# First-layer matmuls in alternation with the second layer of the preceding block, on a recurrence followed by a max-out MLP

## Chip, cores, metric

One Trainium2 chip, one core. The metric is the device time of one execution in microseconds (us), as a median of several runs. The kernel before took 483.24 us (482.63 to 483.64, 4 runs). All runs that are compared here were in the same, fast state with the matmul clock granted almost in full (a mean of 0.994 to 1.0 in every run), so nothing below depends on the clock.

## The reference

```python
# x, f_logit: [4, 6144, 256];  lower_bound: [256];  w1, w2: [256, 1024];  w_out: [1024, 256]
f = lower_bound + (1 - lower_bound) * sigmoid(f_logit)
h[t] = f[t] * h[t-1] + (1 - f[t]) * x[t]          # along the 6144 steps; y = all h
out = max(y @ w1, y @ w2) @ w_out                 # 24576 tokens
```

Both kernels use max(a, b) = a + relu(b - a): the output is relu(y @ (w2 - w1)) @ w_out + y @ (w1 @ w_out). The product w1 @ w_out ("w13", 256 x 256) is made once. I call y @ (w2 - w1) the **hidden** matmuls, y @ w13 the **base** matmuls, and the rest the **projection**.

## The kernel before

PE is the engine that does the matmuls, ACT the one for activations, DVE the vector engine. PSUM is the memory that matmuls write to; each kernel divides up eight banks of it. N is the number of columns that one matmul makes.

The kernel works on 48 blocks of 512 tokens. Per block PE does 16 transposes (x and f_logit come with tokens on the partitions, the recurrence needs them along the free dimension), 16 hidden matmuls (8 tiles dT of 128 x 512, two matmuls each), 8 base matmuls and 32 projection matmuls of N=256. ACT makes the sigmoid and, for each dT tile, the relu that frees the tile's PSUM buffer. DVE makes the gates, the scan and the copy of the output out of PSUM.

```python
    ps_t = ctx.enter_context(tc.tile_pool(name="ps_t", bufs=2, space=bass.MemoryType.PSUM))
    ps_d = ctx.enter_context(tc.tile_pool(name="ps_d", bufs=2, space=bass.MemoryType.PSUM))
    ps_o = ctx.enter_context(tc.tile_pool(name="ps_o", bufs=1, space=bass.MemoryType.PSUM))
    # ... (cut)
    def recurrence(j):
        # ... per half h of the 256 channels: 8 transposes into tT, then
            u = midpool.tile([P, TB], BF16, name="u")
            nc.scalar.activation(out=u[:], in_=fT, func=AF.Sigmoid, scale=-1.0)      # L174
            # ... ff = 1 + u * (lb - 1)                                              # L176
            nc.vector.scalar_tensor_tensor(out=v[:], in0=u[:], scalar=om[:, h : h + 1],
                in1=xT, op0=ALU.mult, op1=ALU.mult)                                  # L185
            # ... y = scan(ff, v)                                                    # L195

    def moe(j, w21, wob, w13b):
        # ...
        for fc in range(FC):                                       # 8 dT tiles
            dT = ps_d.tile([P, TB], FP32, name="dT")
            for kc in range(KC):
                nc.tensor.matmul(dT[:, :], lhsT=w21[:, kc, fc * P : (fc + 1) * P],
                    rhs=yk[kc][:, :], start=(kc == 0), stop=(kc == KC - 1))          # L213
            rt = rpool.tile([P, TB], BF16, name="rt")
            nc.scalar.activation(out=rt[:], in_=dT[:], func=AF.Relu)                 # L221
            rts.append(rt)
        psos = [ps_o.tile([P, D], FP32, name=f"psO{i}") for i in range(NSB)]   # 4 banks
        # ... base matmuls into psos                                                 # L226
        # ... projection: for fc, for i: psos[i] += rts[fc][:, i].T @ wob[fc]        # L235
        # ... one copy per psO, one store per pair                                   # L245

    for j in range(NBLK):
        if j + 2 < NBLK:
            load_nat(blocks[j + 2])
        if j + 1 < NBLK:
            recurrence(j + 1)
        moe(j, w21, wob, w13b)
```

PE's order inside this program is chosen by the scheduler; it puts the base matmuls between the hidden ones.

## Time and profile before

| what | value | view |
|---|---|---|
| time, span of the profiled run | 483.24 us, 481.1 us | runs, page |
| PE / DVE / ACT busy | 93% / 62% / 56% | page, part 1 |
| period of one block | 9.46 us (first osb copy 202.29, next block's 211.75) | timeline |
| PE work in a block, from starts of matmuls that wait for nothing | 16 x 0.2157 + 40 x 0.109 + 16 x 0.056 = 8.71 us | timeline |
| first hidden matmul, last matmul | 22.77 us, 476.28 us | timeline |

PE's 93% is no measure of how much is left. The Trainium skill, "Perfetto Trace Analysis", section "Identifying the Most-Contended Engine", says that matmul busy time is not a good measure of the distance to the limit, because pipelined instructions look smaller in a trace. The conclusion holds here, but in this trace they look longer: a matmul of N=512 is recorded as 0.38 us long, and the next one starts 0.215 us later. So count starts, not lengths.

The page of the kernel before: busy time, the chain that ended last, and groups (line, engine, operation, tiles | busy us, mean ns | idle before, releaser).

```profile
PE 448.3 (93%) x3440; PEld 309.0 (64%) x3488; DVE 296.2 (62%) x486; ACT 267.1 (56%) x500; POOL 71.9 (15%) x102
...
PE 65%; ACT 21%; issue 5%; DVE 5%; DMA 3%; SPq 0%; ACTq 0%; DVEq 0%
PE dT L213 27%; ACT rt L221 11%; ACT u L174 10%; DVE osb L245 4%; DMA won<-in_moe_w_out_dram 3%; PE dT L109 1%; PE psO_1331 L235 0%; PE psO_5231 L235 0%; PE psO_5101 L235 0%; PE psO_4971 L235 0%; PE psO_4451 L235 0%; PE psO_2631 L235 0%; PE
...
L221 ACT ACTIVATE rt<-dT 128x512 bf16<-128x512 f32 x384 | 214.2, 600 | 37.8 <-PE dT L213 36.9
...
L174 ACT ACTIVATE u<-tT 128x512 bf16<-128x512 bf16 x96 | 52.2, 595 | 153.9 <-DVE osb L245 150.0
...
L185 DVE SCALAR_TENSOR_TENSOR v<-u,om,tT 128x512 bf16<-128x512 bf16 x96 | 69.4, 723 | 0.0
```

The chain of work that ended last is 65% PE but 21% ACT: ACT is on the critical path although it is busy only 56% of the time.

The timeline of one hidden stage of the kernel before (start, duration, engine, line, instruction):

```profile
203.52 0.38 PE L213 MATMUL dT<-y_2586,w_144 128*128 128x512 bf16 x1
...
203.96 0.38 PE L213 MATMUL dT<-y_2586,w_144 128*128 128x512 bf16 x1
...
204.08 1.09 ACT L221 ACTIVATE rt<-dT 128x512 bf16<-128x512 f32 x2
204.17 0.27 PE L226 MATMUL psO_2758<-w13b,y_2569 128*128 128x256 bf16 x1
...
204.39 0.27 PE L226 MATMUL psO_2759<-w13b,y_2569 128*128 128x256 bf16 x1
...
204.74 0.38 PE L213 MATMUL dT<-y_2569,w_144 128*128 128x512 bf16 x1
```

PE starts hidden matmuls 0.215 us apart up to 203.96 (two of four are shown; the first has no record in the trace), then three base matmuls 0.11 us apart, the last at 204.39. That one is over at 204.50, but the next hidden matmul starts at 204.74: its dT tile is the third, and there are two buffers. The first relu (of the two in the 204.08 line) is what it waits for: it ends at 204.08 + 0.60 = 204.68. There are four such holes in this stage, of 0.24, 0.07, 0.19 and 0.26 us. They make up the 9.46 - 8.71 = 0.75 us per block. No bracket marks them behind PE, because a matmul is recorded longer than it holds up the next (a base matmul 0.27 us, a hidden one 0.38) and covers most of the hole after it. In the list of waits they stand with the weight loads, which waited for something that the profile does not name ("issue"):

```profile
engine line waited for: us in total, times, longest us
PEld L213 <- issue: 44.8, 192, 0.5
```

A table of one block (us of the stretch, then busy us and number of instructions of each engine, clock, DMA share, GB/s):

```profile
core 0: us, PE busy (x) PEld busy (x) DVE busy (x) ACT busy (x) POOL busy (x), PEclk, DMA share, GB/s
202.29:211.75 9.46, 9.20 (x73) 6.33 (x73) 6.08 (x11) 5.43 (x10) 1.48 (x2) 1.00 0.68 112
```

### The profile page before, as it was taken

The numbers are of one execution on the slowest core, as the hardware profiler recorded it, in microseconds if no ns is written. First come the engines' busy times: TensorE is split into PE (matmuls) and PEld (weight loads), VectorE is DVE, ScalarE is ACT, GpSimd is POOL, SyncE is SP. The second block draws the span as 40 slices with busy tenths as digits, with TensorE's granted clock in tenths as the row PEclk, the third lists the DMA queues.
The fourth block names the chain that finished last, engine by engine and source line by source line (L and its number), as shares of the span: only waits on it lengthen the run. The fifth ranks groups of instructions, "written<-read, shape, count | busy, mean of one in ns | idle before, by whom it ended". The sixth has DMA issues, their size and how long they took to land.

```text
span 481.1 us, 8867 instructions
## 1 busy us (share of the span) xinstructions
PE 448.3 (93%) x3440; PEld 309.0 (64%) x3488; DVE 296.2 (62%) x486; ACT 267.1 (56%) x500; POOL 71.9 (15%) x102
## 2 busy tenths in 40 slices
PE   0799999999999999999999999999999999999996
PEld 0566766676677667666766776676667666766663
DVE  2576577556756765676577567656765665577461
ACT  1666466546655664566466546655664565466553
POOL 4211121112111211211121112111111211120000
PEclk9999999999999999999999999999999999999999
DMA  9957567756765775677567757765785677465112
GB/s 246 191 99 121 90 119 120 113 87 131 118 104 89 136 119 96 102 138 111 90 124 115 114 89 133 118 102 99 130 122 90 120 116 116 89 115 106 46 45 87
DMA packets 78698, 54.06 MB, mean 112 GB/s; under 512 B 3392, under 2 KB 78144, under 8 KB 78656
## 3 DMA queue, kind: packets, MB, share of 16 engines
q0 software_dynamic: 50688, 25.17, 43.4%
q1 hardware_dynamic: 27968, 28.32, 19.6%
q8 instruction: 27, 0.44, 0.4%
q14 instruction: 15, 0.12, 0.1%
HBM read 53.48 MB, written 25.17 MB: 163 GB/s over the span
## 4 chain that ended last, share of the span: by engine, by line
PE 65%; ACT 21%; issue 5%; DVE 5%; DMA 3%; SPq 0%; ACTq 0%; DVEq 0%
PE dT L213 27%; ACT rt L221 11%; ACT u L174 10%; DVE osb L245 4%; DMA won<-in_moe_w_out_dram 3%; PE dT L109 1%; PE psO_1331 L235 0%; PE psO_5231 L235 0%; PE psO_5101 L235 0%; PE psO_4971 L235 0%; PE psO_4451 L235 0%; PE psO_2631 L235 0%; PE psO_1981 L235 0%; PE psO_4321 L235 0%; PE psO_2111 L235 0%
## 5 line engine op out<-in xcount | busy, mean ns | idle before, releaser
L221 ACT ACTIVATE rt<-dT 128x512 bf16<-128x512 f32 x384 | 214.2, 600 | 37.8 <-PE dT L213 36.9
L235 PEld LDWEIGHTS <-rt 128*128 128x128 bf16 x1536 | 150.0, 98 | 27.7
L174 ACT ACTIVATE u<-tT 128x512 bf16<-128x512 bf16 x96 | 52.2, 595 | 153.9 <-DVE osb L245 150.0
L213 PEld LDWEIGHTS <-w_144 128*128 128x128 bf16 x768 | 72.3, 97 | 81.8 <-issue 44.8
L140 POOL DMA_DIRECT2D xn<-in_x_dram x48 | 35.7, 744 | 356.3 <-PE tT L168 349.4
L185 DVE SCALAR_TENSOR_TENSOR v<-u,om,tT 128x512 bf16<-128x512 bf16 x96 | 69.4, 723 | 0.0
L162 PE MATMUL tT<-ident_b,xn 128*128 128x128 bf16 x384 | 37.5, 222 | 12.2 <-DMA xn<-in_x_dram 11.4
L176 DVE TENSOR_SCALAR ff<-u,lbm_94 128x512 bf16<-128x512 bf16 x96 | 46.3, 483 | 3.1 <-ACT u L174 1.6
L168 PE MATMUL tT<-ident_b,fn 128*128 128x128 bf16 x384 | 37.7, 221 | 1.2 <-DMA fn<-in_f_logit_dram 1.2
L162 PEld LDWEIGHTS <-xn 128*128 128x128 bf16 x384 | 27.9, 99 | 13.4 <-DMA xn<-in_x_dram 11.4
L144 POOL DMA_DIRECT2D fn<-in_f_logit_dram x48 | 35.9, 749 | 3.6 <-PE tT L168 2.3
L168 PEld LDWEIGHTS <-fn 128*128 128x128 bf16 x384 | 25.9, 99 | 1.5 <-DMA fn<-in_f_logit_dram 1.4
L101 ACT COPY w1T<-dT 128x128 bf16<-128x128 bf16 x16 | 3.0, 298 | 10.9 <-PE dT L94 10.9
L245 DVE COPY osb<-psO_6356 128x256 f32<-128x256 f32 x1 | 0.4, 425 | 7.2 <-PE psO_6356 L235 7.2
L79 DVE TENSOR_TENSOR w_144<-w2n,w1n 128x2048 bf16<-128x2048 f32 x1 | 2.3, 2293 | 2.7 <-DMA w2n<-in_moe_w_dram 2.7
L87 DVE CAST wob<-won 128x2048 bf16<-128x2048 f32 x1 | 1.2, 1228 | 3.8 <-DMA won<-in_moe_w_out_dram 3.8
L94 PE MATMUL dT<-ident_b,w1b 128*128 128x128 bf16 x16 | 2.2, 306 | 1.3 <-ACT w1T L101 1.2
L213 PE MATMUL dT<-y_121,w_144 128*128 128x512 bf16 x8 | 3.0, 377 | 0.3 <-ACT rt L221 0.2
L81 DVE CAST w1b<-w1n 128x2048 bf16<-128x2048 f32 x1 | 1.2, 1226 | 3.2 <-DMA w1n<-in_moe_w_dram 3.2
L213 PE MATMUL dT<-y_1269,w_144 128*128 128x512 bf16 x7 | 2.6, 377 | 0.5 <-ACT rt L221 0.4
L213 PE MATMUL dT<-y_5039,w_144 128*128 128x512 bf16 x7 | 2.6, 377 | 0.5 <-ACT rt L221 0.4
L213 PE MATMUL dT<-y_1286,w_144 128*128 128x512 bf16 x8 | 3.0, 378 | 0.1
(1066 smaller groups left out, 1034.3 us busy)
## 6 DMA issues: line engine op xcount, KB each, us to landing
out_dram<-osb SPq DMA_DIRECT2D x96, 256.0 KB, 2.4
xn<-in_x_dram POOLq DMA_DIRECT2D x48, 256.0 KB, 5.5
fn<-in_f_logit_dram POOLq DMA_DIRECT2D x48, 256.0 KB, 6.1
w1n<-in_moe_w_dram SPq DMA_DIRECT2D x1, 1024.0 KB, 5.2
w2n<-in_moe_w_dram SPq DMA_DIRECT2D x1, 1024.0 KB, 8.8
won<-in_moe_w_out_dram SPq DMA_DIRECT2D x1, 1024.0 KB, 14.4
lbc<-in_lower_bound_dram SPq DMA_DIRECT2D x1, 1.0 KB, 2.1
```

Source lines behind the costliest of these rows:

```text
L109: nc.tensor.matmul(psw[:, 0:D], lhsT=w1T[:, fc, kc * P : (kc + 1) * P], rhs=wob[:, fc, :], start=(fc == 0), stop=(fc == FC - 1),)
L140: nc.gpsimd.dma_start(out=xn[:], in_=x[blk.b, blk.t0 : blk.t0 + TB, :].rearrange("(i p) d -> p i d", p=P),)
L144: nc.gpsimd.dma_start(out=fn[:], in_=f_logit[blk.b, blk.t0 : blk.t0 + TB, :].rearrange("(i p) d -> p i d", p=P),)
L162: nc.tensor.transpose(tT[:, i * TSB : (i + 1) * TSB], blk.xn[:, i, h * P : (h + 1) * P], ident_b[:],)
L168: nc.tensor.transpose(tT[:, TB + i * TSB : TB + (i + 1) * TSB], blk.fn[:, i, h * P : (h + 1) * P], ident_b[:],)
L174: nc.scalar.activation(out=u[:], in_=fT, func=AF.Sigmoid, scale=-1.0)
L176: nc.vector.tensor_scalar(out=ff[:], in0=u[:], scalar1=lbm1[:, h : h + 1], scalar2=1.0, op0=ALU.mult, op1=ALU.add,)
L185: nc.vector.scalar_tensor_tensor(out=v[:], in0=u[:], scalar=om[:, h : h + 1], in1=xT, op0=ALU.mult, op1=ALU.mult,)
L213: nc.tensor.matmul(dT[:, :], lhsT=w21[:, kc, fc * P : (fc + 1) * P], rhs=yk[kc][:, :], start=(kc == 0), stop=(kc == KC - 1),)
L221: nc.scalar.activation(out=rt[:], in_=dT[:], func=AF.Relu)
L235: nc.tensor.matmul(psos[i][:, :], lhsT=rts[fc][:, i * TSB : (i + 1) * TSB], rhs=wob[:, fc, :], start=False, stop=(fc == FC - 1),)
L245: nc.vector.tensor_copy(out=osb[:, r, :], in_=psos[2 * g + r][:, :])
```

## The change

The intent: PE never runs one stage at a time. In each of eight slots it does one dT tile of block j, five matmuls (base or projection) of block j-1 and two transposes of block j+2, so that ACT has the whole slot for a relu. The PE order is fixed by the program. The gate scale (1 - lower_bound) moves out of v into the weights, so v becomes a plain product over both halves; sigmoid and output copy are merged too. Output pairs share a PSUM bank: banks go from 2 + 2 + 4 to 2 + 3 + 3 for transposes, dT and output. Inputs are loaded two blocks at a time, w_out is cast by its load, and weights come in halves from another queue.

The diff, cut to its core:

```diff
-    ps_t = ... bufs=2   ps_d = ... bufs=2   ps_o = ... bufs=1 (four names)
+    ps_t = ... bufs=1 (two names: fT, xT)   ps_d = ... bufs=3   ps_o = ... bufs=3 (one name)
 # recurrence: one instruction over both halves
-            nc.scalar.activation(out=u[:], in_=fT, func=AF.Sigmoid, scale=-1.0)      # 128x512, twice
-            nc.vector.scalar_tensor_tensor(out=v[:], in0=u[:], scalar=om[:, h : h + 1], in1=xT, ...)
+        nc.scalar.activation(out=u[:], in_=fT[:], func=AF.Sigmoid, scale=-1.0)       # 128x1024  L113
+        nc.vector.tensor_tensor(out=v[:], in0=u[:], in1=xT[:], op=ALU.mult)          # 128x1024  L115
 # weights
-        nc.vector.tensor_tensor(out=w21[:], in0=w2n[:], in1=w1n[:], op=ALU.subtract)
+            nc.vector.tensor_tensor(out=wdf[:, :, cols], in0=w2n[...], in1=w1n[...], op=ALU.subtract)
+                nc.vector.tensor_scalar_mul(out=wd[:, kc, cols], in0=wdf[:, kc, cols], scalar1=om[:, kc : kc + 1])
-            nc.scalar.copy(out=w13b[:, kc, :], in_=psw[:, 0:D])
+            nc.scalar.mul(w13[:, kc, :], psw[:, 0, :], om[:, kc : kc + 1])
+    def project(j, slot):      # slot = token tile i, half of its 10 matmuls
+        i, half = divmod(slot, 2)
+        g, r = divmod(i, 2)
+        ...
+        steps = [(y[:, kc, tok], w13[:, kc, :]) for kc in range(KC)]
+        steps += [(rts[j, fc][:, tok], wob[:, fc, :]) for fc in range(FC)]
+        for s in range(half * n // 2, (half + 1) * n // 2):
+            nc.tensor.matmul(ps[:, r, :], lhsT=steps[s][0], rhs=steps[s][1],          # L227
+                start=(r == 0 and s == 0), stop=(r == 1 and s == n - 1), skip_group_check=True)
+        # after the pair: one copy 128x512 (L237), one store
-    for j in range(NBLK):
-        load_nat(blocks[j + 2]); recurrence(j + 1); moe(j, w21, wob, w13b)
+    with tc.manual_schedule(engines={ENG.PE}):
+        for j in range(NBLK + 1):
+            ... load(c) four blocks ahead
+            for fc in range(FC):
+                if j < NBLK:
+                    hidden(j, fc)          # 2 matmuls, then relu (L202, L210)
+                if j > 0:
+                    project(j - 1, fc)     # 5 matmuls
+                if j + 2 < NBLK:
+                    turn(j + 2, fc)        # 2 transposes (L103)
+            if j + 2 < NBLK:
+                recurrence(j + 2)
```

Two outputs in one PSUM bank need care with the start flag: only the first matmul into the bank carries it. The Trainium skill, "PSUM — Partial Sum Buffer", section "The four PSUM rules", describes this idiom ("`first_mm` only on the first matmul issued in that bank × quadrant").

More of the change, by code (lines that the diff above doesn't have):

```diff
@@ L13 @@
 AF = mybir.ActivationFunctionType
+ENG = mybir.EngineType
 P = 128
@@ L36 @@
     TB = 512
-    TSB = 128
-    NSB = TB // TSB
-    assert S % TB == 0
-    NBLK_PER_B = S // TB
-    NBLK = B * NBLK_PER_B
+    NSB = TB // P
+    CH = 2 * TB
+    assert S % CH == 0
+    NBB = S // TB
+    NBLK = B * NBB
+    chunks = [(0, 1), (1, 1)] + [(j, 2) for j in range(2, NBLK, 2)]
+    home = {j + o: (c, o) for c, (j, n) in enumerate(chunks) for o in range(n)}
     const = ctx.enter_context(tc.tile_pool(name="const", bufs=1))
     wpool = ctx.enter_context(tc.tile_pool(name="wpool", bufs=1))
-    natpool = ctx.enter_context(tc.tile_pool(name="nat", bufs=3))
+    inpool = ctx.enter_context(tc.tile_pool(name="inp", bufs=4))
     midpool = ctx.enter_context(tc.tile_pool(name="mid", bufs=2))
     ypool = ctx.enter_context(tc.tile_pool(name="ypool", bufs=4))
-    rpool = ctx.enter_context(tc.tile_pool(name="rpool", bufs=10))
-    opool = ctx.enter_context(tc.tile_pool(name="opool", bufs=3))
-    ps_t = ctx.enter_context(tc.tile_pool(name="ps_t", bufs=2, space=bass.MemoryType.PSUM))
-    ps_d = ctx.enter_context(tc.tile_pool(name="ps_d", bufs=2, space=bass.MemoryType.PSUM))
-    ps_o = ctx.enter_context(tc.tile_pool(name="ps_o", bufs=1, space=bass.MemoryType.PSUM))
+    rpool = ctx.enter_context(tc.tile_pool(name="rpool", bufs=2 * FC + 4))
+    opool = ctx.enter_context(tc.tile_pool(name="opool", bufs=4))
+    ps_t = ctx.enter_context(
+        tc.tile_pool(name="ps_t", bufs=1, space=bass.MemoryType.PSUM)
+    )
+    ps_d = ctx.enter_context(
+        tc.tile_pool(name="ps_d", bufs=3, space=bass.MemoryType.PSUM)
+    )
+    ps_o = ctx.enter_context(
+        tc.tile_pool(name="ps_o", bufs=3, space=bass.MemoryType.PSUM)
+    )
     ident_f = const.tile([P, P], FP32)
@@ L57 @@
     nc.vector.tensor_copy(out=ident_b[:], in_=ident_f[:])
+    om = const.tile([P, KC], FP32)
+    nom = const.tile([P, KC], FP32)
     lbc = const.tile([P, KC], FP32)
     nc.sync.dma_start(out=lbc[:], in_=lower_bound.rearrange("(h p) -> p h", p=P))
-    lbm1 = const.tile([P, KC], FP32)
-    nc.vector.tensor_scalar_add(out=lbm1[:], in0=lbc[:], scalar1=-1.0)
-    om = const.tile([P, KC], FP32)
     nc.vector.tensor_scalar(
-        out=om[:],
-        in0=lbc[:],
-        scalar1=-1.0,
-        scalar2=1.0,
-        op0=ALU.mult,
-        op1=ALU.add,
-    )
+        out=om[:], in0=lbc[:], scalar1=-1.0, scalar2=1.0, op0=ALU.mult, op1=ALU.add
+    )
@@ new lines, with load @@
+    nc.vector.tensor_scalar_add(out=nom[:], in0=lbc[:], scalar1=-1.0)
+    ins = {}
+    def load(c):
+        j, n = chunks[c]
+        b, k = divmod(j, NBB)
+        t0, nt = k * TB, n * TB
+        ni = nt // P
+        tiles = []
+        for name, src in (("fn", f_logit), ("xn", x)):
+            nat = inpool.tile([P, CH // P, D], BF16, name=name)
+            nc.gpsimd.dma_start(
+                out=nat[:, 0:ni, :],
+                in_=src[b, t0 : t0 + nt, :].rearrange("(i p) d -> p i d", p=P),
+            )
+            tiles.append(nat)
+        ins[c] = tiles
@@ new lines, with turn, recurrence @@
+    ys = {}
+    turned = {}
+    def turn(j, slot):
+        c, o = home[j]
+        s, q = divmod(slot, FC // 2)
+        if q == 0:
+            turned[j, s] = ps_t.tile([P, KC, TB], BF16, name=("fT", "xT")[s])
+        dst = turned[j, s]
+        for h in range(KC):
+            nc.tensor.transpose(
+                dst[:, h, q * P : (q + 1) * P],
+                ins[c][s][:, o * NSB + q, h * P : (h + 1) * P],
+                ident_b[:],
+            )
+    def recurrence(j):
+        fT, xT = turned[j, 0], turned[j, 1]
+        prev = ys.get(j - 1) if j % NBB else None
+        u = midpool.tile([P, KC, TB], BF16, name="u")
+        nc.scalar.activation(out=u[:], in_=fT[:], func=AF.Sigmoid, scale=-1.0)
+        v = midpool.tile([P, KC, TB], BF16, name="v")
+        nc.vector.tensor_tensor(out=v[:], in0=u[:], in1=xT[:], op=ALU.mult)
+        ff = midpool.tile([P, KC, TB], BF16, name="ff")
+        y = ypool.tile([P, KC, TB], BF16, name="y")
+        for h in range(KC):
+            nc.vector.tensor_scalar(
+                out=ff[:, h, :],
+                in0=u[:, h, :],
+                scalar1=nom[:, h : h + 1],
+                scalar2=1.0,
+                op0=ALU.mult,
+                op1=ALU.add,
+            )
+            nc.vector.tensor_tensor_scan(
+                out=y[:, h, :],
+                data0=ff[:, h, :],
+                data1=v[:, h, :],
+                initial=0.0 if prev is None else prev[:, h, TB - 1 : TB],
+                op0=ALU.mult,
+                op1=ALU.add,
+            )
+        ys[j] = y
@@ L73, in weight_prep @@
     def weight_prep():
         w1n = wpool.tile([P, KC, DFF], FP32)
-        nc.sync.dma_start(out=w1n[:], in_=moe_w1.rearrange("(kc p) f -> p kc f", p=P))
         w2n = wpool.tile([P, KC, DFF], FP32)
-        nc.sync.dma_start(out=w2n[:], in_=moe_w2.rearrange("(kc p) f -> p kc f", p=P))
-        w21 = wpool.tile([P, KC, DFF], BF16)
-        nc.vector.tensor_tensor(out=w21[:], in0=w2n[:], in1=w1n[:], op=ALU.subtract)
+        wob = wpool.tile([P, FC, D], BF16)
         w1b = wpool.tile([P, KC, DFF], BF16)
-        nc.vector.tensor_copy(out=w1b[:], in_=w1n[:])
@@ L82, in weight_prep @@
-        won = wpool.tile([P, FC, D], FP32)
-        nc.sync.dma_start(
-            out=won[:], in_=moe_w_out.rearrange("(fc p) c -> p fc c", p=P)
-        )
-        wob = wpool.tile([P, FC, D], BF16)
-        nc.vector.tensor_copy(out=wob[:], in_=won[:])
+        wdf = wpool.tile([P, KC, DFF], FP32)
+        wd = wpool.tile([P, KC, DFF], BF16)
+        for g in range(2):
+            cols = slice(g * DFF // 2, (g + 1) * DFF // 2)
+            for w, src in ((w1n, moe_w1), (w2n, moe_w2)):
+                nc.scalar.dma_start(
+                    out=w[:, :, cols],
+                    in_=src[:, cols].rearrange("(kc p) f -> p kc f", p=P),
+                )
@@ new lines, in weight_prep @@
+        nc.gpsimd.dma_start(
+            out=wob[:], in_=moe_w_out.rearrange("(fc p) c -> p fc c", p=P)
+        )
+        for g in range(2):
+            cols = slice(g * DFF // 2, (g + 1) * DFF // 2)
+            nc.scalar.copy(out=w1b[:, :, cols], in_=w1n[:, :, cols])
+            nc.vector.tensor_tensor(
+                out=wdf[:, :, cols],
+                in0=w2n[:, :, cols],
+                in1=w1n[:, :, cols],
+                op=ALU.subtract,
+            )
+            for kc in range(KC):
+                nc.vector.tensor_scalar_mul(
+                    out=wd[:, kc, cols], in0=wdf[:, kc, cols], scalar1=om[:, kc : kc + 1]
+                )
@@ L91, in weight_prep @@
                 pt = ps_d.tile([P, TB], BF16, name="dT")
-                for j in range(4):
-                    fc = 4 * g + j
+                for q in range(4):
+                    fc = 4 * g + q
                     nc.tensor.transpose(
-                        pt[:, j * P : (j + 1) * P],
+                        pt[:, q * P : (q + 1) * P],
                         w1b[:, kc, fc * P : (fc + 1) * P],
@@ L98, in weight_prep @@
                     )
-                for j in range(4):
-                    fc = 4 * g + j
-                    nc.scalar.copy(
-                        out=w1T[:, fc, kc * P : (kc + 1) * P],
-                        in_=pt[:, j * P : (j + 1) * P],
-                    )
-        w13b = wpool.tile([P, KC, D], BF16)
+                nc.scalar.copy(
+                    out=w1T[:, 4 * g : 4 * g + 4, kc * P : (kc + 1) * P],
+                    in_=pt[:].rearrange("p (q d) -> p q d", q=4),
+                )
+        w13 = wpool.tile([P, KC, D], BF16)
         for kc in range(KC):
-            psw = ps_d.tile([P, TB], FP32, name="dT")
+            psw = ps_o.tile([P, 2, D], FP32, name="psO")
             for fc in range(FC):
                 nc.tensor.matmul(
-                    psw[:, 0:D],
+                    psw[:, 0, :],
                     lhsT=w1T[:, fc, kc * P : (kc + 1) * P],
@@ L115, in weight_prep @@
                 )
-            nc.scalar.copy(out=w13b[:, kc, :], in_=psw[:, 0:D])
-        return w21, wob, w13b
-    class Blk:
-        pass
-    blocks: list = []
-    for b in range(B):
-        for c in range(NBLK_PER_B):
-            blk = Blk()
-            blk.b = b
-            blk.c = c
-            blk.t0 = c * TB
-            blocks.append(blk)
-    def out_rows(blk, i0, n):
-        r0 = blk.b * S + blk.t0 + i0 * TSB
-        return out[r0 : r0 + n * TSB, :].rearrange("(i p) d -> p i d", p=P)
@@ L135 @@
-    ys = {}
-    def load_nat(blk):
-        xn = natpool.tile([P, NSB, D], BF16, name="xn")
-        fn = natpool.tile([P, NSB, D], BF16, name="fn")
-        nc.gpsimd.dma_start(
-            out=xn[:],
-            in_=x[blk.b, blk.t0 : blk.t0 + TB, :].rearrange("(i p) d -> p i d", p=P),
-        )
-        nc.gpsimd.dma_start(
-            out=fn[:],
-            in_=f_logit[blk.b, blk.t0 : blk.t0 + TB, :].rearrange(
-                "(i p) d -> p i d", p=P
-            ),
-        )
-        blk.xn = xn
-        blk.fn = fn
@@ L153, in recurrence @@
-    def recurrence(j):
-        blk = blocks[j]
-        prev = ys.get(j - 1) if blk.c > 0 else None
-        yh = []
-        for h in range(KC):
-            tT = ps_t.tile([P, 2 * TB], BF16, name="tT")
-            xT = tT[:, 0:TB]
-            fT = tT[:, TB : 2 * TB]
-            for i in range(NSB):
-                nc.tensor.transpose(
-                    tT[:, i * TSB : (i + 1) * TSB],
-                    blk.xn[:, i, h * P : (h + 1) * P],
-                    ident_b[:],
-                )
-            for i in range(NSB):
-                nc.tensor.transpose(
-                    tT[:, TB + i * TSB : TB + (i + 1) * TSB],
-                    blk.fn[:, i, h * P : (h + 1) * P],
-                    ident_b[:],
-                )
-            u = midpool.tile([P, TB], BF16, name="u")
-            nc.scalar.activation(out=u[:], in_=fT, func=AF.Sigmoid, scale=-1.0)
-            ff = midpool.tile([P, TB], BF16, name="ff")
-            nc.vector.tensor_scalar(
-                out=ff[:],
-                in0=u[:],
-                scalar1=lbm1[:, h : h + 1],
-                scalar2=1.0,
-                op0=ALU.mult,
-                op1=ALU.add,
-            )
-            v = midpool.tile([P, TB], BF16, name="v")
-            nc.vector.scalar_tensor_tensor(
-                out=v[:],
-                in0=u[:],
-                scalar=om[:, h : h + 1],
-                in1=xT,
-                op0=ALU.mult,
-                op1=ALU.mult,
-            )
-            y = ypool.tile([P, TB], BF16, name=f"y{h}")
-            init = 0.0 if prev is None else prev[h][:, TB - 1 : TB]
-            nc.vector.tensor_tensor_scan(
-                out=y[:],
-                data0=ff[:],
-                data1=v[:],
-                initial=init,
-                op0=ALU.mult,
-                op1=ALU.add,
-            )
-            yh.append(y)
-        ys[j] = tuple(yh)
@@ L206, in moe @@
-    def moe(j, w21, wob, w13b):
-        blk = blocks[j]
-        yk = ys[j]
-        rts = []
-        for fc in range(FC):
-            dT = ps_d.tile([P, TB], FP32, name="dT")
-            for kc in range(KC):
-                nc.tensor.matmul(
-                    dT[:, :],
-                    lhsT=w21[:, kc, fc * P : (fc + 1) * P],
-                    rhs=yk[kc][:, :],
-                    start=(kc == 0),
-                    stop=(kc == KC - 1),
-                )
-            rt = rpool.tile([P, TB], BF16, name="rt")
-            nc.scalar.activation(out=rt[:], in_=dT[:], func=AF.Relu)
-            rts.append(rt)
-        psos = [ps_o.tile([P, D], FP32, name=f"psO{i}") for i in range(NSB)]
-        for i in range(NSB):
-            for kc in range(KC):
-                nc.tensor.matmul(
-                    psos[i][:, :],
-                    lhsT=yk[kc][:, i * TSB : (i + 1) * TSB],
-                    rhs=w13b[:, kc, :],
-                    start=(kc == 0),
-                    stop=False,
-                )
-        for fc in range(FC):
-            for i in range(NSB):
-                nc.tensor.matmul(
-                    psos[i][:, :],
-                    lhsT=rts[fc][:, i * TSB : (i + 1) * TSB],
-                    rhs=wob[:, fc, :],
-                    start=False,
-                    stop=(fc == FC - 1),
-                )
-        for g in range(NSB // 2):
-            osb = opool.tile([P, 2, D], FP32, name="osb")
-            for r in range(2):
-                nc.vector.tensor_copy(out=osb[:, r, :], in_=psos[2 * g + r][:, :])
-            nc.sync.dma_start(out=out_rows(blk, 2 * g, 2), in_=osb[:])
@@ L248, with hidden @@
-    load_nat(blocks[0])
-    if NBLK > 1:
-        load_nat(blocks[1])
-    recurrence(0)
-    w21, wob, w13b = weight_prep()
-    for j in range(NBLK):
-        if j + 2 < NBLK:
-            load_nat(blocks[j + 2])
-        if j + 1 < NBLK:
-            recurrence(j + 1)
-        moe(j, w21, wob, w13b)
+            nc.scalar.mul(w13[:, kc, :], psw[:, 0, :], om[:, kc : kc + 1])
+        return wd, wob, w13
+    rts = {}
+    def hidden(j, fc):
+        y = ys[j]
+        dT = ps_d.tile([P, TB], FP32, name="dT")
+        for kc in range(KC):
+            nc.tensor.matmul(
+                dT[:],
+                lhsT=wd[:, kc, fc * P : (fc + 1) * P],
+                rhs=y[:, kc, :],
+                start=(kc == 0),
+                stop=(kc == KC - 1),
+            )
+        rt = rpool.tile([P, TB], BF16, name="rt")
+        nc.scalar.activation(out=rt[:], in_=dT[:], func=AF.Relu)
+        rts[j, fc] = rt
@@ new lines @@
+    pos = {}
+    def project(j, slot):
+        i, half = divmod(slot, 2)
+        g, r = divmod(i, 2)
+        y = ys[j]
+        if r == 0 and half == 0:
+            pos[j] = ps_o.tile([P, 2, D], FP32, name="psO")
+        ps = pos[j]
+        tok = slice(i * P, (i + 1) * P)
+        steps = [(y[:, kc, tok], w13[:, kc, :]) for kc in range(KC)]
+        steps += [(rts[j, fc][:, tok], wob[:, fc, :]) for fc in range(FC)]
+        n = len(steps)
+        for s in range(half * n // 2, (half + 1) * n // 2):
+            nc.tensor.matmul(
+                ps[:, r, :],
+                lhsT=steps[s][0],
+                rhs=steps[s][1],
+                start=(r == 0 and s == 0),
+                stop=(r == 1 and s == n - 1),
+                skip_group_check=True,
+            )
+        if r == 1 and half == 1:
+            osb = opool.tile([P, 2, D], FP32, name="osb")
+            nc.vector.tensor_copy(out=osb[:], in_=ps[:])
+            r0 = j * TB + 2 * g * P
+            nc.sync.dma_start(
+                out=out[r0 : r0 + 2 * P, :].rearrange("(r p) d -> p r d", p=P),
+                in_=osb[:],
+            )
@@ new lines @@
+    started = {c: chunks[c][0] for c in range(len(chunks))}
+    ahead = 4
+    for c in range(len(chunks)):
+        if started[c] < ahead:
+            load(c)
+    for slot in range(FC):
+        turn(0, slot)
+    recurrence(0)
+    wd, wob, w13 = weight_prep()
+    for slot in range(FC):
+        turn(1, slot)
+    recurrence(1)
+    with tc.manual_schedule(engines={ENG.PE}):
+        for j in range(NBLK + 1):
+            for c in range(len(chunks)):
+                if started[c] == j + ahead:
+                    load(c)
+            for fc in range(FC):
[7 more added lines that the diff above has]
+                recurrence(j + 2)
```

## The prediction

> **What bounds the kernel now.** The page gives PE 93% busy, DVE 62%, ACT 56%. The timeline around 202 us shows a period of 9.46 us per 512-token block (first osb copy at 202.29, the next block's at 211.75), 48 of them from the first L213 matmul at 22.77 us to the last L235 matmul at 476.28 us. PE starts matmuls 0.215 us apart at N=512 (L213), 0.109 us at N=256 (L226, L235) and 0.056 us in the transposes (L162/L168), in agreement with the Trainium skill, "TensorE: Matmul & The Clock Gate", section "Wait — 56ns, not 53.3ns?" (215.7 and 55.6 ns warm). So a block holds 16 x 0.2157 + 40 x 0.109 + 16 x 0.056 = 8.71 us of PE work. The other 0.75 us are holes in the L213 stage (204.50 to 204.74, 205.88 to 206.07, 207.15 to 207.41 and so on), where the next dT tile waits for one of two PSUM buffers: ACT's relu ends one every 0.55 us, PE fills one in 0.43. The chain of waits agrees: PE dT L213 27%, ACT rt L221 11%, ACT u L174 10%. The scheduler already puts the eight L226 matmuls into the holes; they don't fill them.
>
> **What the change does.** Matmuls, transposes and bytes stay the same (6978 PE rows in both orders). PE's order is now fixed: per slot 2 hidden matmuls, 5 projection matmuls of the block before, 2 transposes: 0.43 + 0.545 + 0.11 = 1.09 us per relu of 0.55 us, with three dT buffers. In ACT's order the merged sigmoid (1024 columns, estimated 1.0 us) follows the fourth relu, just when its fT is complete. ACT needs about 5.4 us per block, DVE about 5.9 (two scans of 1.25, two copies of 0.65, two ff of 0.34, one v of 1.2), both far below 8.7; y, xT and psO have half a block of slack. So PE should not run dry: the saving is 48 x 0.75 = 36 us, all on the critical path. Fewer DVE and ACT instructions, the folded scale and the larger DMAs are off it and worth nothing by themselves.
>
> **Head.** DMA decides it. Before, won landed at 16.6 us. After, w13 no longer precedes the first hidden matmul, but wob is queued behind 2 MB (as bf16) of inputs; at the 196 GB/s that the windows from 16 to 22 us show for this queue alone I estimate it lands near 22 us. ident_b is cast after the second weight difference, near 12 us, so the transposes start there, y(0) is ready near 18.5, the first hidden matmul near 18.6; w13 runs inside block 0. First hidden to last projection: 48 x (16 x 0.2157 + 40 x 0.109) + 46 x 0.9 = 416 us, plus 3 to 4 for w13 and its wait: PE ends near 438.5. Tail: before 4.8 us; now one merged copy, about 4.3. Span 443; the measured time was 2 above the span: 445 us. Range 439 to 454.
>
> **Right if the profile shows** a period of 8.7 us; PE idle before hidden matmuls near zero; ACT and DVE busy near 5.4 and 5.9 us per block; first hidden matmul at 17 to 21 us; w13 waiting for wob at 21 to 25 us.
>
> **What would make it wrong.** (a) Weight loads not hidden where matmuls of different N alternate: 0.02 us per slot is 8 us. (b) A wait in every block on fT or xT, which have one buffer each. (c) wob landing at 30 us, +7 us. (d) Larger input DMAs colliding with output. None reaches 36 us.
>
> Chances: faster by over 2% 0.97, within 2% 0.02, slower 0.01. Predicted 445 us, 439 to 454.

## The result

The changed kernel took 445.10 us (444.91 to 445.16, 4 runs) against 483.24 us. The ratio is 0.9209, 95% interval 0.9196 to 0.9222. The outputs are right. (Ratios are the mean time of one kernel's fast runs over that of the other's of the same rounds, so not quite the ratio of the medians quoted.)

The page of the changed kernel, the same parts:

```profile
PE 423.0 (95%) x3488; PEld 309.8 (70%) x3488; DVE 247.0 (56%) x345; ACT 278.5 (63%) x442; POOL 44.9 (10%) x57
...
PE 94%; DMA 4%; POOL 1%; DVE 0%; issue 0%; POOLq 0%
PE psO L227 47%; PE dT L202 37%; PE xT L103 5%; PE fT L103 5%; DMA wob<-in_moe_w_out_dram 4%; POOL fn L86 1%; POOL xn L86 1%; PE psO L186 0%; DVE osb L237 0%; POOL ident_f masks.py:199 0%; POOL ident_f masks.py:197 0%; POOLq masks.py:199 0%
...
L210 ACT ACTIVATE rt<-dT 128x512 bf16<-128x512 f32 x384 | 226.8, 597 | 142.2 <-PE dT L202 142.1
...
L115 DVE TENSOR_TENSOR v<-u,xT 128x1024 bf16<-128x1024 bf16 x48 | 32.5, 677 | 3.9 <-PE xT L103 3.9
```

ACT has left the chain (the idle time that the sigmoid line of before showed, 153.9 us, was mostly in the projection stage and cost nothing by itself): it is now 94% PE, and what remains (DMA 4%) is the head. The relu's mean is unchanged (600 before, 597 ns now), and ACT is now idle before it, waiting for PE. The weight loads' share (PEld) rose with unchanged total: they tell the gain better than PE's 93% to 95%.

The timeline where a block of the changed kernel is half done, one slot and the start of the next (the first line is the relu of the slot before):

```profile
205.22 0.60 ACT L210 ACTIVATE rt<-dT 128x512 bf16<-128x512 f32 x1 [0.49 <-PE dT L202]
...
205.51 0.28 PE L103 MATMUL fT<-ident_b,fn 128*128 128x128 bf16 x2
...
205.62 0.59 PE L202 MATMUL dT<-y,wd 128*128 128x512 bf16 x2
...
205.87 1.02 ACT L113 ACTIVATE u<-fT 128x1024 bf16<-128x1024 bf16 x1
206.05 0.38 PE L227 MATMUL psO<-w_182,y 128*128 128x256 bf16 x2
...
206.59 0.28 PE L103 MATMUL xT<-ident_b,xn 128*128 128x128 bf16 x2
...
206.71 0.59 PE L202 MATMUL dT<-y,wd 128*128 128x512 bf16 x2
206.79 1.15 ACT L210 ACTIVATE rt<-dT 128x512 bf16<-128x512 f32 x2
```

Transposes at 205.51, hidden matmuls at 205.62, five matmuls of the block before from 206.05, the next transposes at 206.59, the next hidden matmuls at 206.71. One slot takes 206.71 - 205.62 = 1.09 us, which is its PE work: 2 x 0.2157 + 5 x 0.109 + 2 x 0.056. There is no room for a hole. A relu starts about 0.69 us after its matmuls (204.53 to 205.22 in the slot before), so this tile's was due near 206.3; it starts only at 206.79, because the sigmoid of 1.02 us is in front of it. PE doesn't notice.

One whole block of the changed kernel, between copies of like pairs:

```profile
201.35:210.06 8.71, 8.71 (x75) 6.38 (x73) 5.12 (x7) 5.65 (x10) 0.88 (x1) 1.00 0.37 78
```

The period is 8.71 us, DVE has 5.1 us and ACT 5.65 us of work in it. All the waits of PE in the whole execution:

```profile
PE fT L103 <- DVE ident_b L65: 13.4, 1, 13.4
PE psO L186 <- DMA wob<-in_moe_w_out_dram: 1.8, 1, 1.8
PE dT L202 <- DVE y L127: 1.1, 2, 0.7
```

And those of the weight loads, which showed the holes before, less the one for the first input:

```profile
PEld L103 <- issue: 3.3, 2, 2.3
PEld L186 <- issue: 2.1, 1, 2.1
PEld L202 <- DVE y L127: 0.5, 1, 0.5
```

All of these are in the head; the 44.8 us are gone. Where the 37.8 us of span went, by three points in the two timelines:

| stretch | before | after | difference |
|---|---|---|---|
| start to first hidden matmul | 22.77 | 18.02 | -4.75 |
| to the last block's last copy start | 453.5 (to 476.26, the first of four) | 421.3 (to 439.30) | -32.2 |
| to the end of the span | 4.8 | 4.0 | -0.8 |

The middle stretch is 48 x 0.75 = 36 us shorter, less 3.7 us for w13, which has moved into it (1.83 us wait for wob, 1.91 us of matmuls).

### The profile page after: what moved, and what is told of

Same layout as the page of the kernel before. It is cut to its first block, busy times and chain, and to the rows that moved or that the text cites. A ratio compares the mean times of both kernels' runs of the same rounds, so it can differ in the third digit from the quotient of the medians.

```text
span 443.3 us, 8434 instructions
## 1 busy us (share of the span) xinstructions
PE 423.0 (95%) x3488; PEld 309.8 (70%) x3488; DVE 247.0 (56%) x345; ACT 278.5 (63%) x442; POOL 44.9 (10%) x57
## 4 chain that ended last, share of the span: by engine, by line
PE 94%; DMA 4%; POOL 1%; DVE 0%; issue 0%; POOLq 0%
PE psO L227 47%; PE dT L202 37%; PE xT L103 5%; PE fT L103 5%; DMA wob<-in_moe_w_out_dram 4%; POOL fn L86 1%; POOL xn L86 1%; PE psO L186 0%; DVE osb L237 0%; POOL ident_f masks.py:199 0%; POOL ident_f masks.py:197 0%; POOLq masks.py:199 0%; POOLq L284 0%
## 5 line engine op out<-in xcount | busy, mean ns | idle before, releaser
L227 PE MATMUL psO<-wob,rt 128*128 128x256 bf16 x1536 | 229.8, 273 | 0.0
L202 PE MATMUL dT<-y,wd 128*128 128x512 bf16 x768 | 228.2, 379 | 1.1 <-DVE y L127 1.1
L237 DVE COPY osb<-psO 128x512 f32<-128x512 f32 x96 | 66.4, 692 | 152.5 <-PE psO L227 152.5
L127 DVE TENSOR_TENSOR_SCAN y<-ff,y,v 128x512 bf16<-128x512 bf16 x88 | 108.2, 1272 | 1.5
L227 PE MATMUL psO<-w_182,y 128*128 128x256 bf16 x384 | 73.3, 273 | 0.0
L227 PEld LDWEIGHTS <-y 128*128 128x128 bf16 x384 | 37.6, 98 | 44.4
L103 PE MATMUL fT<-ident_b,fn 128*128 128x128 bf16 x384 | 52.2, 221 | 13.4 <-DVE ident_b L65 13.4
L202 PEld LDWEIGHTS <-wd 128*128 128x128 bf16 x768 | 59.6, 98 | 0.9 <-DVE y L127 0.5
L103 PE MATMUL xT<-ident_b,xn 128*128 128x128 bf16 x384 | 52.2, 221 | 0.0
L113 ACT ACTIVATE u<-fT 128x1024 bf16<-128x1024 bf16 x48 | 49.1, 1024 | 4.9 <-PE fT L103 2.3
```

Source lines behind the costliest of these rows:

```text
L103: nc.tensor.transpose(dst[:, h, q * P : (q + 1) * P], ins[c][s][:, o * NSB + q, h * P : (h + 1) * P], ident_b[:],)
L113: nc.scalar.activation(out=u[:], in_=fT[:], func=AF.Sigmoid, scale=-1.0)
L127: nc.vector.tensor_tensor_scan(out=y[:, h, :], data0=ff[:, h, :], data1=v[:, h, :], initial=0.0 if prev is None else prev[:, h, TB - 1 : T ...
L202: nc.tensor.matmul(dT[:], lhsT=wd[:, kc, fc * P : (fc + 1) * P], rhs=y[:, kc, :], start=(kc == 0), stop=(kc == KC - 1),)
L227: nc.tensor.matmul(ps[:, r, :], lhsT=steps[s][0], rhs=steps[s][1], start=(r == 0 and s == 0), stop=(r == 1 and s == n - 1), skip_group_che ...
L237: nc.vector.tensor_copy(out=osb[:], in_=ps[:])
```

## Experiments

The steady state was predicted well, but two explanations give the same number. **Mine:** PE stands still when the PE time between a dT tile and the one that takes over its buffer is shorter than ACT needs to empty it; the alternation stretches that time. **The rival:** the shared PSUM banks pay, because they make room for a third dT buffer, and the alternation is decoration. Others: PE at 93% was bound by its work all along; the folding and merging on DVE and ACT pay; the fixed order pays; the head pays.

All twelve, beside the two kernels, with the period from the timelines ("hole" is the period less 8.71 us):

| run | what | time us | ratio to before | period | hole |
|---|---|---|---|---|---|
| before | one block at a time, 2 dT buffers | 483.3 | 1 | 9.46 | 0.75 |
| b3m | same, 3 dT buffers | 463.7 | 0.959 | 9.08 | 0.37 |
| b4m | same, 4 dT buffers | 446.1 | 0.922 | 8.71 | 0 |
| b3man | same, 3, base matmuls spread | 445.9 | 0.922 | 8.71 | 0 |
| changed | alternation, 3 | 445.1 | 0.921 | 8.71 | 0 |
| a_d2 | alternation, 2 | 445.7 | 0.922 | 8.71 | 0 |
| a_burst | alternation undone, 3 | 459.2 | 0.950 | 9.01 | 0.30 |
| a_burst_d2 | alternation undone, 2 | 513.5 | 1.062 | 10.16 | 1.45 |
| b_now13 | before, no base matmuls (wrong) | 480.7 | 0.994 | 9.41 | |
| a_now13 | changed, no base matmuls (wrong) | 403.1 | 0.834 | 7.84 | |
| a_unfold | changed, folding and merging undone | 445.5 | 0.922 | 8.71 | 0 |
| a_sched | changed, scheduler orders PE | 444.8 | 0.921 | 8.71 | 0 |
| a_ident | changed, earlier identity | 446.0 | 0.923 | 8.71 | 0 |
| a_head | changed, head reordered | 443.0 | 0.917 | 8.71 | 0 |

### b_now13: work taken away from the kernel before

```diff
-                nc.tensor.matmul(psos[i][:, :], lhsT=yk[kc][...], rhs=w13b[:, kc, :], ...)   # 8 a block
-                    start=False,
+                    start=(fc == 0),                       # projection
-    for j in range(NBLK): ...
+    with tc.manual_schedule(engines={mybir.EngineType.PE}):   # keeps the rest of the order
+        for j in range(NBLK): ...
```

> Wrong on purpose: the kernel before without the eight base matmuls (y times w13) of a block, rest of the PE order fixed as it was. They are 48 x 8 x 0.109 = 42 us of PE work. Theory: in the kernel before they sit in holes that ACT and two dT buffers make, so taking them away only widens the holes: 476 to 484 us. Rival (PE at 93% busy is bound by its work): about 441 us.

Measured: 480.67 us, ratio 0.9939 (0.9922 to 0.9956). Of 42 us of PE work, 2.6 us came off. So the hidden stage of the kernel before, where these matmuls stand, was not bound by PE's work (in the projection stage PE starts a matmul every 0.109 us without a hole). The timeline of this run, from one block's copies to the next:

```profile
202.02 1.42 DVE L236 COPY osb<-psO 128x256 f32<-128x256 f32 x4 [3.25 <-PE psO L226]
...
205.16 1.09 ACT L221 ACTIVATE rt<-dT 128x512 bf16<-128x512 f32 x2 [0.25 <-PE dT L213]
205.81 1.08 PE L213 MATMUL dT<-y,w 128*128 128x512 bf16 x4 [0.26 <-ACT rt L221]
...
206.50 1.09 ACT L221 ACTIVATE rt<-dT 128x512 bf16<-128x512 f32 x2 [0.25 <-PE dT L213]
...
207.83 1.09 ACT L221 ACTIVATE rt<-dT 128x512 bf16<-128x512 f32 x2 [0.25 <-PE dT L213]
...
211.43 1.42 DVE L236 COPY osb<-psO 128x256 f32<-128x256 f32 x4 [3.25 <-PE psO L226]
```

With nothing else in the stage the loop stands bare. Two relus run back to back (1.09 us for both), then ACT waits 0.25 us for PE; PE fills two tiles (4 matmuls, 1.08) and waits 0.26 us for ACT. The relu pairs start at 205.16, 206.50 and 207.83: two buffers give two tiles per 1.33 us, neither engine at its own pace. PE could fill two in 0.86 us. The time is a buffer's round trip: 0.69 us from the first matmul of a tile to its relu (205.81 to 206.50), 0.60 us of relu, and 0.04 us until PE starts the tile that takes the buffer over (207.14). That is 1.33 us, and two buffers allow two tiles in it.

### a_now13: the same work taken away from the changed kernel

```diff
-        steps = [(y[:, kc, tok], w13[:, kc, :]) for kc in range(KC)]
-        steps += [(rts[j, fc][:, tok], wob[:, fc, :]) for fc in range(FC)]
+        steps = [(rts[j, fc][:, tok], wob[:, fc, :]) for fc in range(FC)]
```

> Wrong on purpose: the changed kernel without the eight base matmuls of a block, 48 x 8 x 0.109 = 42 us of PE work. Theory (PE's own work is now the only bound): 401 to 406 us. The same matmuls taken from the kernel before gave 2.6 us. Rival (another engine or DMA is close behind): above 415.

Measured: 403.06 us, 42 us less than the changed kernel. The same eight matmuls cost 2.6 us before and 42 us after: the bound has moved from the loop of PE and ACT to PE's own work. No other engine and no DMA came in the way within these 42 us.

### b3m and b4m: more dT buffers in the old order

```diff
-        psos = [ps_o.tile([P, D], FP32, name=f"psO{i}") for i in range(NSB)]
+        pairs = [ps_o.tile([P, 2, D], FP32, name=f"psO{g}") for g in range(NSB // 2)]
+        psos = [pairs[i // 2][:, i % 2, :] for i in range(NSB)]
 # start only on the first matmul into each pair's bank; one copy per pair
-    ps_d = ... bufs=2
+    ps_d = ... bufs=3        # b3m;  4 in b4m
```

> The kernel before with psO pairs sharing a bank and, from the banks freed, a third dT buffer; nothing else. The scheduler then puts all eight L213 pairs back to back and the base matmuls after them. My theory (what counts is that the PE time between one dT tile and the third after it covers ACT's 0.55 us per relu): the last tile of a block waits for the fifth relu, a hole of about 0.65 us per block remains, period about 9.4 us, time 476 to 482 us. Rival (the change gained because of the third dT buffer alone): period 8.7, about 448 us.

> The same with four dT buffers. Theory: the last tile waits for the fourth relu only, a hole of 0.1 to 0.2 us per block, period 8.8 to 8.9, time 451 to 457 us: buffers alone, if there are enough, do nearly all that the alternation does. Rival (matmuls of another block are needed to fill the stage): stays above 470.

Measured: 463.7 us (ratio 0.959) and 446.1 us (0.9224). Both figures of mine for b3m and b4m were too slow, and the rival's for b3m too fast. Copies, relus and the last weight load of a stage, with three buffers:

```profile
204.22 1.29 DVE L247 COPY osb<-psO 128x512 f32<-128x512 f32 x2 [3.03 <-PE psO L237]
...
205.90 4.03 ACT L221 ACTIVATE rt<-dT 128x512 bf16<-128x512 f32 x8
...
208.52 0.10 PEld L213 LDWEIGHTS <-w 128*128 128x128 bf16 x1 [0.18 <-issue]
...
213.30 1.29 DVE L247 COPY osb<-psO 128x512 f32<-128x512 f32 x2 [3.03 <-PE psO L237]
```

and the copies with four:

```profile
204.04 1.29 DVE L247 COPY osb<-psO 128x512 f32<-128x512 f32 x2 [2.67 <-PE psO L237]
...
212.75 1.29 DVE L247 COPY osb<-psO 128x512 f32<-128x512 f32 x2 [2.66 <-PE psO L237]
```

Eight relus in a row take 4.03 us, so they start (4.03 - 0.60) / 7 = 0.49 us apart, not 0.55. I had halved the 1.09 us of a pair, which is 0.49 + 0.60. The Trainium skill, "ScalarE: Activation LUTs", section "What ACT_TABLE_LOAD costs", says that back-to-back ACTIVATEs overlap by about 93 ns; here it is 0.60 - 0.49 = 0.11 us. With the right pace b3m comes out: the eighth tile needs the fifth relu, which ends at 205.90 + 4 x 0.49 + 0.60 = 208.46, and the eighth tile's weights load at 208.52. With four buffers it needs only the fourth relu, and the hole is gone: the old order, with four dT buffers, is as fast as the changed kernel in the steady state. In this the rival is right further than I thought: the shared banks could have done it alone, if spent on dT.

### b3man: three buffers, the base matmuls spread by hand

```diff
             rts.append(rt)
+            i, kc = divmod(fc, KC)
+            nc.tensor.matmul(psos[i], lhsT=yk[kc][:, i * TSB : (i + 1) * TSB], rhs=w13b[:, kc, :],
+                start=(i % 2 == 0 and kc == 0), stop=False, skip_group_check=True)
-        (the loop of base matmuls after the stage)
+    with tc.manual_schedule(engines={mybir.EngineType.PE}): (around the loop over blocks)
```

> Three dT buffers and a fixed PE order inside one block: one base matmul after each hidden pair, projection after the stage, no alternation with the preceding block. Theory: a tile then costs PE 0.54 us against ACT's 0.55, so the holes close to under 0.1 us per block: 447 to 451 us. Rival (alternation of two blocks is what matters): 470 or more.

Measured: 445.91 us, ratio 0.9219. Its copies are 8.71 us apart:

```profile
204.45 1.29 DVE L246 COPY osb<-psO 128x512 f32<-128x512 f32 x2 [2.66 <-PE psO L236]
...
213.16 1.29 DVE L246 COPY osb<-psO 128x512 f32<-128x512 f32 x2 [2.67 <-PE psO L236]
```

In b3m the scheduler, given a third buffer, stopped filling the stage with base matmuls and put all hidden matmuls back to back; with the order set by hand three buffers are enough and no other block's work is needed. PE's 0.54 us per tile is then above the relu pace of 0.49.

### a_d2, a_burst, a_burst_d2: buffers against order

```diff
-        tc.tile_pool(name="ps_d", bufs=3, ...)
+        tc.tile_pool(name="ps_d", bufs=2, ...)       # a_d2, a_burst_d2
             for fc in range(FC):
                 if j < NBLK:
                     hidden(j, fc)
+            for fc in range(FC):                     # a_burst, a_burst_d2
                 if j > 0:
                     project(j - 1, fc)
+            for fc in range(FC):
                 if j + 2 < NBLK:
                     turn(j + 2, fc)
```

> The changed kernel with two dT buffers in place of three, order unchanged. Theory: in the alternation a dT buffer is wanted again 2.2 us (two slots) after it was filled, and relu with its latency and a sigmoid in front takes at most 1.9: no hole, 444 to 447 us. Rival (the third buffer from the shared banks is what pays, as the four-buffer run of the old order suggests): 455 or more.

> The changed kernel with the alternation undone and three dT buffers kept: all hidden matmuls of a block, then all projections of the block before, then all transposes. Theory, with the relu pace of 0.49 us that the first four runs showed: the last tile waits for the fifth relu, hole 0.3 to 0.5 us per block: 459 to 469 us. Rival (order does not matter once banks are shared and the stages are of different blocks): 445.

> The same with two dT buffers. Theory: a fill and its relu then form a loop of 1.33 us per two tiles as in the kernel before without base matmuls, hole 1.3 to 1.6 us per block: 507 to 522 us, slower than the kernel before. With the run of two buffers in alternation this shows what the order is worth when buffers are short. Rival: 465 or less.

Measured: 445.68, 459.15 and 513.52 us, all as my theory had it (a_burst at the lower end of its range). In alternation the third buffer is worth nothing; the list of waits of a_d2 has, in the whole execution, one wait of PE for a relu and three of hidden weight loads, all before 28 us:

```profile
PE dT L202 <- ACT rt L210: 0.2, 1, 0.2
```

```profile
PEld L202 <- issue: 0.6, 3, 0.3
```

Without the alternation and with two buffers the changed kernel is 6% slower than the kernel before. Its timeline from one second-pair copy to the next:

```profile
199.71 0.69 DVE L237 COPY osb<-psO 128x512 f32<-128x512 f32 x1 [1.49 <-PE psO L227]
...
201.13 1.08 ACT L210 ACTIVATE rt<-dT 128x512 bf16<-128x512 f32 x2
...
201.77 1.08 PE L202 MATMUL dT<-y,wd 128*128 128x512 bf16 x4 [0.34 <-ACT rt L210]
...
202.40 1.09 ACT L210 ACTIVATE rt<-dT 128x512 bf16<-128x512 f32 x2 [0.19 <-PE dT L202]
...
209.87 0.69 DVE L237 COPY osb<-psO 128x512 f32<-128x512 f32 x1 [1.49 <-PE psO L227]
```

The same loop as in b_now13, with the sigmoid in front. So the alternation is worth 513.5 - 445.7 = 68 us with two buffers, 459.2 - 445.1 = 14 us with three, and, as b4m shows for the old order, nothing with four (the changed kernel was not run with the alternation undone and four buffers).

### a_unfold: the work on DVE and ACT put back

```diff
-        nc.scalar.activation(out=u[:], in_=fT[:], func=AF.Sigmoid, scale=-1.0)
-        nc.vector.tensor_tensor(out=v[:], in0=u[:], in1=xT[:], op=ALU.mult)
+        for h in range(KC): nc.scalar.activation(out=u[:, h, :], in_=fT[:, h, :], ...)
+        for h in range(KC): nc.vector.scalar_tensor_tensor(out=v[:, h, :], ..., scalar=om[:, h : h + 1], ...)
-                nc.vector.tensor_scalar_mul(out=wd[...], in0=wdf[...], scalar1=om[:, kc : kc + 1])
+                nc.vector.tensor_scalar_mul(out=wd[...], in0=wdf[...], scalar1=1.0)
-            nc.scalar.mul(w13[:, kc, :], psw[:, 0, :], om[:, kc : kc + 1])
+            nc.scalar.copy(out=w13[:, kc, :], in_=psw[:, 0, :])
-            nc.vector.tensor_copy(out=osb[:], in_=ps[:])
+            (two copies, one per half)
```

> The changed kernel with the folded scale and the merged instructions undone: gate scale back in v (one scalar_tensor_tensor per half), two sigmoids, two copies per output pair, weights unscaled. Theory: this work is off the critical path in every block; DVE busy rises by about 1 us per block and the time stays within 1 us of the changed kernel: 444 to 446.5 us. Rival (the folding and merging paid part of the 38 us): 450 or more.

Measured: 445.47 us, ratio 0.9221 (0.9208 to 0.9233); the changed kernel's is 0.9209. One block of it:

```profile
201.35:210.06 8.71, 8.66 (x74) 6.36 (x73) 5.82 (x10) 5.65 (x11) 0.96 (x1) 1.00 0.30 70
```

DVE went from 5.12 to 5.82 us in the block (I had expected about 1 us more) and the period stayed at 8.71. The folded scale and the merged instructions saved work, but none of it was waited for.

### a_sched: without the fixed order

```diff
-    with tc.manual_schedule(engines={ENG.PE}):
+    if True:
```

> The changed kernel without the fixed PE order: the program lists the alternation, the scheduler orders PE. Its PE order then differs from the fixed one in the first block only. Theory: 444 to 447 us. Rival (the fixed order is needed): 455 or more.

Measured: 444.79 us, ratio 0.9206 (0.9194 to 0.9219). Once the program lists the alternation, the scheduler keeps it; the two PE orders differ in the first block only. The fixing is not what pays.

### a_ident and a_head: the head

```diff
-    nc.vector.tensor_copy(out=ident_b[:], in_=ident_f[:])
+    nc.scalar.copy(out=ident_b[:], in_=ident_f[:])                      # a_ident and a_head
-    chunks = [(0, 1), (1, 1)] + [(j, 2) for j in range(2, NBLK, 2)]
+    chunks = [(j, 1) for j in range(4)] + [(j, 2) for j in range(4, NBLK, 2)]    # a_head from here
-    (all chunks of the first four blocks loaded, then the weights)
+    (chunks 0 to 2 loaded, then the weights, then chunk 3)
-        (w13 computed before block 0)
+            if j == 0: (w13 computed at the end of block 0)
```

> The changed kernel with the cast of ident_b moved from DVE, where it stood behind the second weight difference (13.1 us), to ACT. Theory: the first transposes start when fn lands, near 11 us, and the first hidden matmul comes about 2 us earlier, but PE then waits that much longer for wob at 23.5 us: time within 1 us of the changed kernel, 444 to 446. Rival (the head is bound by y(0)): 442 to 443.

> ident_b on ACT, chunk 2 split into two one-block loads with wob queued between them, and the w13 matmuls moved to the end of block 0. Theory: wob lands near 21 us and w13 no longer waits for it, the 1.8 us wait and the 2 us of late transposes both go: 440 to 442.5 us. Rival (the inputs of block 2 or 3 then come too late): 445 or more.

Measured: a_ident 445.95 us (0.9231, 0.9214 to 0.9248; two runs took 445.2 us and two 446.7), a_head 443.03 us (0.917, 0.9157 to 0.9182). In the changed kernel the identity for the transposes was ready at 13.38 us though fn had landed at 10.99. Having it earlier brought nothing: in a_ident PE starts w13 at 23.67 us, against 23.51 in the changed kernel, because wob lands no sooner. Only with wob moved forward in the queue and w13 moved back does the head get shorter. Of the waits of PE in a_head, the one for y(0) and the one for a relu:

```profile
PE dT L205 <- DVE y L127: 1.4, 2, 0.7
...
PE dT L205 <- ACT rt L213: 0.3, 1, 0.3
```

The wait for wob is gone. I expected 440 to 442.5 us and got 443.0, a miss: of the 2 us of late transposes only 1.1 came off. The first two hidden matmuls start at 16.95 and 18.05 us, against 18.02 and 19.13 in the changed kernel, since block 0's x landed only at 12.7 us and y(0) was still waited for (1.4 us). Against a_sched, a_head is 1.8 us faster, and it is the fastest correct version: it beats both kernels.

## Why the prediction was right

**What bounded the kernel before: right.** The holes of 0.75 us per block in the hidden stage were read from the timeline and put down to two dT buffers. b_now13 (42 us of PE work removed, 2.6 us gained) and b3m, b4m (holes 0.37 and 0 with more buffers) show it.

**The pace in that explanation: mis-sized.** The prediction says "ACT's relu ends one every 0.55 us". It is 0.49 us in a row, and 1.33 us per two tiles in the loop of two buffers, which the 0.25 us that each engine waits for the other makes slower than either. This did not touch the predicted time, since the saving was taken as period less PE work. It did spoil the expectations for b3m, b4m and b3man, which ran 12, 5 and 1 us below the lower ends of the ranges that I had given.

**The saving of 48 x 0.75 = 36 us: right.** The period is 8.71 us as predicted, and the trace shows no wait of PE after the head. Alternating N=128, 256 and 512 cost no extra time for weight loads: a slot takes the 1.09 us that was worked out.

**What causes the saving: right, but the prediction did not ask what else would.** It named three dT buffers and the order in one breath. a_d2 shows that the order alone is enough, b4m that buffers alone are, b3man that three buffers and base matmuls spread within the block are.

**"Worth nothing by themselves": right** for the folded scale and the merged instructions (a_unfold). For the larger input loads it was not tested alone; the split of one of them in a_head was tied to other edits. But b4m and b3man reach the period of 8.71 us with the one-block loads of the kernel before, so that period doesn't need them.

**ACT and DVE load: small misses off the path.** ACT has 5.65 us of work per block where 5.4 was estimated, DVE 5.1 where 5.9 was. On DVE the term that was off is v, estimated 1.2 us and measured 0.68 us (below); the terms that the prediction lists also add up to 5.7 and not 5.9. On ACT it is again the relu, taken as 0.55 us: in the alternation most relus start alone and take 0.60.

**Head: right within 1.5 us.** First hidden matmul 18.02 us (18.6 predicted; its second half at 19.13, after the second half of y(0)). wob was awaited until 23.51 us where it was estimated to land near 22; w13 cost 1.83 us of waiting and 1.91 of work, 3 to 4 predicted. The profiled span is 443.3 us, 443 predicted.

## What to carry to other kernels

When a matmul result is emptied by another engine through n buffers, compare two times: how long the matmul engine is busy from one tile to the tile that reuses its buffer, and how long the other engine needs, with its queue and the latencies, to empty it. If the first is shorter, there is a hole. In this kernel more buffers, or other work spread between the tiles, closed it equally well (b4m, a_d2, b3man), so choose by what is scarce: PSUM or a simple program. To learn whether an engine at 93% is bound by its work, take work away: here 42 us of it was worth 2.6 us before the change and 42 us after.

## What the Trainium skill lacked or had wrong

- "VectorE: DVE Perf Modes", section "The perf-mode tier table (the rule you actually need)", gives 1× for `tensor_tensor` with any operand in PSUM. Here v, 128 x 1024 bf16 with xT in PSUM, takes 677 ns; at one element per cycle of the page's 0.96 GHz it could not be under 1067 ns. The page's own section "Why PSUM operands drop a tier" (2×_1P at most, 1× for fp32) fits the measurement. The `scalar_tensor_tensor` that it replaced took 723 ns for half the elements.
- "Perfetto Trace Analysis", section "Optimization Strategy", says that the same gap repeating on an engine "can mean there isn't enough SBUF/PSUM for the next tile to be allocated", and advises interleaving regimes. Both hold here. It does not say that the two are substitutes, or how many buffers it takes: 483.3, 463.7 and 446.1 us with 2, 3 and 4 dT buffers in the old order; 445.7 and 445.1 with 2 and 3 in alternation.
- "TensorE: Matmul & The Clock Gate" gives start-to-start times for runs of one N. Not stated is that mixing them costs nothing: slots of N=512, 256 and 128 matmuls, each with its own weights, take 1.09 us, which is 2 x 0.2157 + 5 x 0.109 + 2 x 0.056.
- "DMA: Bandwidth & Descriptors" has no rate for loads that cast while they move. The windows of the kernel before from 16 to 22 us show 195 to 197 GB/s, counted in the bf16 that lands, when such loads were the only transfers left.
